# A gated attention and feed-forward kernel on one core: half sums, stores and loads become items of the hand-made lists, a left unit moves to another place, left rows of b share the home of left rows of x

## The chip, the cores and the metric

The kernel runs on one core of a Trainium2 chip. Its engines are TensorE (PE; its weight loads are shown apart as PEld), VectorE (DVE), ScalarE (ACT), GpSimd (POOL) and SyncE (SP), which here only issues DMAs. Each engine runs its own instructions in order, and semaphores join them. The metric is device time of one execution in microseconds (us), less is better; the median of three runs of the kernel before is 1715.51 us (1715.17 to 1721.14).

## What is computed

A sequence of 2048 rows of 640 numbers goes through two branches, and a gate for each row mixes them. Branch A is attention in 64 segments of 32 rows, each with 8 memory rows in front; the memory of a segment is what the segment before put out at its first 8 positions. So the segments form a chain. Branch B is a feed-forward block with a gated GELU.

```python
S, Dm, H, Dh, M, seg = 2048, 640, 32, 192, 8, 32
mem = mem0
for s in range(64):
    h = concatenate([mem, x[32*s:32*s+32]])          # 40 rows
    q, k, v = h @ Wq, h @ Wk, h @ Wv                 # 32 heads of 192
    p = softmax(mask(q @ k.T * scale))
    o = (p @ v) @ Wo                                 # 40 x 640
    mem, outs[s] = o[:8], o[8:]
a = concatenate(outs)
b = (gelu(x @ w_gate) * (x @ w_up)) @ w_down
g = sigmoid((x * gate_w).sum(-1))
result = g * a + (1 - g) * b
```

## The kernel before

**Feed-forward first.** Four blocks of 512 rows are computed before the attention. For each block `ffn_gu` runs 12 pairs of matmul groups, ACT does a GELU on each and DVE a product; `gate_block` computes the gate; `ffn_down` runs four row groups of 128. After each row group ACT and DVE move the result from PSUM to one of four buffers `brow`, and ACT issues one DMA that stores 128 rows of b in a scratch tensor in HBM (line 881). In this phase stores, and loads of the first x, are issued by ACT.

**Segments.** A segment has 24 new rows that nothing waits for ("first rows" of x), 8 memory rows from the segment before, and 8 last rows. The last 8 rows of four segments, a group, do not take part in the recurrence as queries of the next segment's memory, so they are the "left" rows: their q and k are computed for four segments at once ("left units", items `lf` and their copying out, `le`), stored in an HBM scratch (`lst store`, line 950, or in halves, line 955) and loaded again for each segment (`stg`, line 1000). Their attention outputs are kept in `uTl` and multiplied with Wo once for each group (`Wol`, at place 3). The four segments of a group are its places 0 to 3, and each place has its own list in `PROGS`.

**Lists.** A list names the order in which work is given to the engines. Heads are taken in four octets, in rising order at even and falling order at odd segments. `g` projects q, k or v of an octet, one of five 128-row pieces of the contraction at a time (each piece and matrix is four matmuls in four column tiles of PE); `tq`, `tk` transpose the rows of q and k on DVE after ACT took them out of PSUM; `sc` computes scores and gives DVE the maximum and the subtraction; `ex` is exp on ACT and sum, reciprocal and product on DVE; `pt` transposes the probabilities on PE; `pv` multiplies with v, and ACT (line 1265), for the last octet also DVE (line 1270), moves the result to `uT`; `wo` multiplies half an octet with Wo; `vb` projects v of the next group's left rows. All engines get their instructions in the order of the list, so an item's place decides what stands in front of what on each engine.

**The end of a segment.** The Wo products of octets 0 to 2 lie in a PSUM bank as two halves on different partitions. `half_sums` moves one half to SBUF on ACT (line 1289) and adds on DVE (two instructions, line 1292); it stands right behind the last of these products. When the last octet's products are done, DVE adds both parts (line 1468) and transposes the memory rows into the next segment's input (line 1472), and the first projection of the next segment waits for that.

**Left rows of u.** POOL copies the 8 left columns of each octet from `uT` to `uTl` (line 1273). So `uT` has 40 columns for each slot, and ACT takes 480 numbers (320 in the last octet) for each partition out of PSUM.

**Weights.** All weights of the attention do not fit in SBUF. Sixteen pairs of pieces share a home; each segment loads the partner of a piece after its use ("swap", line 645), thirteen pieces of 384 KB of Wq, Wk and Wv, one of them only in a part of `HX` bytes for each partition (line 642), and three of 480 KB of Wo. A load is used later in the same segment. All these, and the small loads and stores of a segment, go through SP in the order in which they were given: `out_store` (line 1021) and `x_load` (line 751) behind the last piece of k of octet 1, `bz_load` (line 1012) behind the last projection, four `bzl load` (line 1017), `outl` (line 1026) and so on.

**Names.** `bz` holds b, then the result, of a segment; `bzl` the same of a group's left rows; `XL` the left rows of x; `zpart` and `zsum` are the half sums.

A dependence is found by regions. For PSUM a reader also waits for readers of the same bank on other engines that were given before it.

Of the kernel before, what the change touches and what calls it, by code (L numbers as in the profile page):

```python
# [231 lines left out]
def _build(nc, A_x, A_mem0, A_Wq, A_Wk, A_Wv, A_Wo, seg_len, w_gate, w_up, w_down,  # L232
# [40 lines left out]
    b_scr = nc.dram_tensor("ffn_b_scratch", (S, Dm), BF, kind="Internal").ap()  # L273
    x_scr = nc.dram_tensor("x_scratch", (NSEG, 128, KT * XA), BF, kind="Internal").ap()
# [20 lines left out]
    wsB["bzl"] = al(DJ * 2)  # L295
# [5 lines left out]
    wsB["uT"] = al(NUB * 12 * R * 2)  # L301
# [101 lines left out]
    UB = 12 * R * 2  # L403
    uT = [bview(wsB_off["uT"] + b * UB, UB).rearrange("p (t c r) -> p t c r", c=3, r=R) for b in range(NUB)]
# [7 lines left out]
    bz, bzl = [bview(wsB_off[nm], DJ * 2) for nm in ("bz", "bzl")]  # L412
    Zt = PT[:, 0:DJ]
    r_bzlj = [sreg(wsB_off["bzl"], DJ * 2, 32 * j, 32 * j + 32) for j in range(4)]
# [4 lines left out]
    r_bz, r_bzl = [sreg(wsB_off[nm], DJ * 2) for nm in ("bz", "bzl")]  # L419
# [3 lines left out]
    fp_sz = {"xst": 16 * KT * XA * 2, "xls": 4 * KT * 64, "gr": 512, "gwT": 64}  # L423
# [7 lines left out]
    o_gr = fp_off["gr"]  # L431
# [36 lines left out]
    xls = bview(fp_off["xls"], fp_sz["xls"]).rearrange("p (g c) -> p g c", c=KT * 32)  # L468
    r_xls = sreg(fp_off["xls"], fp_sz["xls"])
    LSB = 4 * 2 * LW * 2  # L470
    lst_off = [fp_off["xst"] + i * LSB for i in range(3)] + [o_ul + 2 * UTQ]
    assert 3 * LSB <= fp_off["gr"] - fp_base
# [36 lines left out]
    def piece_view(key, o):  # L509
        if key[0] == 3:  # L510
# [872 lines left out]
    def segment(s):  # L1383
# [4 lines left out]
        for n, item in enumerate(PROGS[q]):  # L1388
# [57 lines left out]
            if item == gate_at[q]:  # L1446
                gate_now(s)
# [126 lines left out]
```

## Time and profile before

| | us |
|---|---|
| median of three runs | 1715.51 |
| profiled execution, device time | 1721.14 |
| its span, first to last instruction | 1719.3 |
| feed-forward phase and first left units | to about 180 |
| 64 segments | about 180 to 1715 |

The granted clock of TensorE was 0.996 of full speed over the span. The profile's page gives the busy time of each engine, the share of the DMA engines, the chain of waits, and groups of instructions with their mean duration and the idle time in front of them. A view of waits gives who waited for whom in total; a timeline gives instructions in order of time, equal neighbours merged; a view of windows gives busy time in stretches of the span. "ACTq" and "SPq" are the sequencers that issue DMAs. An engine's busy time in PE is modelled: matmuls are pipelined, and a matmul's shown duration is longer than the time after which the next one starts.

### The profile page before, as it was taken

To read this page: it belongs to the slowest core of one execution; us is meant where nothing else is said; L and a number is where in the kernel's file an instruction comes from. 1 tells how busy PE (TensorE), PEld (TensorE's weight loads), DVE (VectorE), ACT (ScalarE), POOL (GpSimd) and SP (SyncE) were. 2 spreads that over 40 slices of the span, in tenths; PEclk is the share of its full clock that TensorE was granted. 3 is DMA by queue.
4 is the path that set the end of the run, shared out by engine and by line. 5 is a ranking of instruction groups with operands and counts; after the bars stand their busy time and mean duration, and the time that the engine had idled before them with its cause. 6 is when DMAs were issued, how large, how long until landed. Compare 5 with 4: busy or idle time off the path is not lost. (4 is left out here: it accounts for less than half of the span.)

```text
span 1719.3 us, 80494 instructions
## 1 busy us (share of the span) xinstructions
PE 1592.6 (93%) x39181; PEld 825.5 (48%) x31501; DVE 956.2 (56%) x2930; ACT 801.1 (47%) x1899; POOL 415.7 (24%) x1101
## 2 busy tenths in 40 slices
PE   9999999999899989899999999899898999899987
PEld 4554445444544445454545445454445445454444
DVE  2222656656565655556565666556565656556554
ACT  3222454545454554545454544445454545445444
POOL 1100222222222222222222222222222222222222
PEclk9999999999999999999999999999999999999999
DMA  9914988978888788888788887879787887879876
GB/s 323 319 53 137 322 299 291 320 278 285 276 303 318 278 293 282 298 304 298 280 280 290 311 299 272 290 280 320 255 288 279 314 312 269 291 265 322 274 275 240
DMA packets 273822, 484.99 MB, mean 282 GB/s; under 512 B 107686, under 2 KB 142782, under 8 KB 273470
## 3 DMA queue, kind: packets, MB, share of 16 engines
q1 hardware_dynamic: 270414, 476.78, 79.2%
q8 instruction: 276, 4.52, 1.0%
q10 hardware_dynamic: 3056, 3.07, 0.5%
q14 instruction: 76, 0.62, 0.1%
HBM read 458.64 MB, written 21.10 MB: 279 GB/s over the span
## 5 line engine op out<-in xcount | busy, mean ns | idle before, releaser
L1121 PE MATMUL ps<-arena 128*32 128x384 bf16 x9940 | 710.8, 329 | 20.6 <-DVE arena L1472 11.8
L226 PE MATMUL ps<-arena 128*32 128x384 bf16 x7680 | 595.3, 327 | 14.3 <-ACT arena L1039 4.4
L1121 PEld LDWEIGHTS ps<-arena 128*32 128x32 bf16 x9940 | 254.7, 96 | 392.7 <-issue 260.6
L1155 DVE STREAM_TRANSPOSE arena<-arena 128x384 bf16<-128x384 bf16 x512 | 275.3, 561 | 151.4 <-ACT arena L1141 149.8
L1141 ACT ACTIVATE arena<-ps 128x384 bf16<-128x384 f32 x512 | 237.1, 490 | 227.0 <-PE ps L1121 212.2
L1283 PE MATMUL ps<-arena 128*32 128x320 bf16 x6144 | 279.7, 301 | 15.5 <-issue 13.2
L1273 POOL COPY arena<-arena 128x96 bf16<-128x96 bf16 x256 | 163.8, 640 | 527.8 <-ACT arena L1265 480.9
L1265 ACT ACTIVATE arena<-ps 128x480 bf16<-128x480 f32 (+1 forms) x256 | 137.5, 537 | 172.3 <-PE ps L1256 160.5
L1283 PEld LDWEIGHTS ps<-arena 128*32 128x32 bf16 x6144 | 169.3, 107 | 72.9 <-issue 23.8
L1006 POOL COPY arena<-arena 128x96 bf16<-128x96 bf16 x256 | 68.9, 269 | 485.4 <-PE ps L1176 387.4
L1144 ACT ACTIVATE arena<-ps 128x384 bf16<-128x384 f32 x256 | 125.2, 489 | 104.9 <-PE ps L1121 101.6
L1189 DVE TENSOR_REDUCE arena<-ps 104x4 f32<-104x160 f32 x256 | 82.8, 323 | 141.9 <-PE ps L1176 125.1
L1203 DVE TENSOR_REDUCE arena<-ps 104x4 f32<-104x160 f32 x256 | 80.9, 316 | 103.8 <-ACT ps L1201 101.5
L1239 ACT ACTIVATE arena<-ps 128x448 bf16<-128x448 f32 x192 | 104.1, 542 | 65.9 <-PE ps L1226 64.9
L1254 PE MATMUL ps<-arena 128*64 128x160 bf16 x1536 | 118.8, 243 | 7.3 <-ACT arena L941 3.2
L1201 ACT ACTIVATE ps<-ps 104x160 f32<-104x160 f32 x256 | 74.8, 292 | 103.0 <-DVE ps L1191 103.0
L1254 PEld LDWEIGHTS ps<-arena 128*64 128x64 bf16 x1536 | 79.8, 109 | 86.4 <-issue 29.9
L936 PE MATMUL ps<-arena 128*32 128x384 bf16 x1280 | 109.4, 327 | 1.1 <-issue 1.1
L1256 PE MATMUL ps<-arena 128*64 128x64 bf16 x1536 | 102.3, 193 | 0.0
L943 DVE STREAM_TRANSPOSE arena<-arena 128x384 bf16<-128x384 bf16 x128 | 73.0, 571 | 44.2 <-ACT arena L941 43.9
L1171 PE MATMUL ps<-arena 128*40 128x40 bf16 x2048 | 68.9, 182 | 26.4 <-DVE arena L1155 24.5
L1306 PE MATMUL ps<-arena 128*32 128x160 bf16 x3072 | 71.7, 233 | 21.7 <-DVE arena L1270 16.4
(85 smaller groups left out, 1824.2 us busy)
## 6 DMA issues: line engine op xcount, KB each, us to landing
arena<-in_A_Wk_dram SPq DMA_DIRECT2D x335, 384.0 KB, 6.7
arena<-in_A_Wv_dram SPq DMA_DIRECT2D x335, 384.0 KB, 8.3
arena<-in_A_Wo_dram SPq DMA_DIRECT2D x205, 480.0 KB, 5.4
arena<-in_A_Wq_dram SPq DMA_DIRECT2D x146, 384.0 KB, 5.2
arena<-left_qk_scratch SPq DMA_DIRECT2D x126, 96.0 KB, 2.1
left_qk_scratch<-arena SPq DMA_DIRECT2D x49, 192.0 KB, 2.8
arena<-in_A_Wq_dram SPq DMA_DIRECT2D x63, 144.0 KB, 3.4
left_qk_scratch<-arena SPq DMA_DIRECT2D x30, 96.0 KB, 3.3
```

What stands on the lines that cost most here:

```text
L226: return e.add_instruction(mybir.InstMatmult(name=nm, start_tensor_calc=like["start"], stop_tensor_calc=stop, tile_size=(128, 32), tile_po ...
L936: fns.append(lambda e, outp=outp, rhs=rhs, j=j: e.matmul(outp, lhs, rhs, start=(k == 0), stop=(k == KT - 1), tile_position=(0, 32 * j)))
L1121: fns.append(lambda e, outp=outp, rhs=rhs, j=j: e.matmul(outp, lhs, rhs, start=(k == 0), stop=(k == KT - 1), tile_position=(0, 32 * j)))
L1141: S_.add("act", lambda e, m=m, bk=bk: e.activation(out=rows_sb[m], in_=ps[:, bk, 0:384], func=ACTF.Copy), reads=[r_ps[bk]], writes=[r_rows ...
L1144: S_.add("act", lambda e, i=i, bk=bk: e.activation(out=v_sb[i % NVB].rearrange("p (c n) -> p c n", c=3), in_=ps[:, bk, 0:384].rearrange("p ...
L1155: S_.add("dve", lambda e: e.transpose(out=dst[:, :, 0:L], in_=rows_sb[m].rearrange("p (c r) -> p c r", r=L)), reads=[r_rows[m]], writes=[r ...
L1239: S_.add("act", lambda e: e.activation(out=PT, in_=ps[:, bank, 0:PTW + 128], func=ACTF.Copy), reads=[r_ps[bank]], writes=[r_PT], name="pT ...
L1254: return [lambda e: e.matmul(full, v[:, e0:e0 + 64], PTm[:, i], start=True, stop=False, tile_position=(0, 64 * i), skip_group_check=True), ...
L1256: lambda e: e.matmul(part, vl[:, e0:e0 + 64], PTl[:, i], start=False, stop=True, tile_position=(0, 64 * i), skip_group_check=True)]
L1265: S_.add("act", lambda e: e.activation(out=apx(u[:, 0, 0, :], [[R, na], [3 * R, 4], [1, R]]), in_=ps[:, A, 0:na * W].rearrange("p (c t r) ...
L1273: S_.add("pool", lambda e: e.tensor_copy(out=uTl[:, q, :, 12 * oc:12 * oc + 12].rearrange("p i (t c) -> p t c i", c=3), in_=u[:, :, :, L:R ...
L1283: fns.append(lambda e, i=i, t=t, j=j, gv=gv: e.matmul(ps[32 * j:32 * j + 32, bank, 0:2 * DJ].rearrange("p (h n) -> p h n", h=2), lhs2[i], ...
```

## The change

1. **uT and uTl.** `uT` keeps 32 columns; ACT takes 384 numbers (256 in the last octet) from PSUM. POOL's copy is gone; DVE copies the left columns from PSUM to `uTl` (96 numbers; in the last octet 64 and 32 from two banks).
2. **bzl in the home of XL.** `bzl` has no home of its own. It is loaded at place 3 behind `("g", 1, 4)`, and the next group's `XL` is loaded at place 0 behind the last projection, once the stores of `bzl` have landed. The left unit of octet 3, which place 0 worked on, is worked on at place 2.
3. **A scratch for left rows of b.** In the feed-forward phase ACT issues four more stores of 8 rows for each row group of 128; `bzl` is then loaded by one DMA in place of four.
4. **The memory that this frees**, with `xls` and the gate's row moved into `brow`, goes to the piece that is loaded in part: `HX` is 384 in place of 1152 bytes for each partition.
5. **New items.** `zp` and `zs` are the two parts of the half sums, `ou` the store of the segment before, `xt` the load of x, `bz` the load of b. `outl` stands at `("sc", 2)` of place 0.
6. **All four lists are new**, with the same kinds of work.

```diff
-    wsB["uT"] = al(NUB * 12 * R * 2)
+    wsB["uT"] = NUB * 12 * L * 2
...
-    HX = 1152
+    HX = 384
...
+            for i in range(4):
+                S_.add(AUXQ, lambda e, bs=bs, row0=row0, i=i: e.dma_start(
+                    bl_scr[row0 // 128, :, M * i:M * i + M].rearrange("j r n -> r j n"),
+                    brow[bs][L * i + XA:L * i + L].rearrange("t (j n) -> t j n", j=4)),
+                    reads=[r_brow[bs]], ..., name="bl store %d" % row0)
...
-    LUNIT = ({1: 3}, {0: 1, 1: 0}, {1: 2}, {})
+    LUNIT = ({}, {0: 1, 1: 0}, {0: 2, 1: 3}, {})
...
     def bzl_load(g):
-        for j in range(4):
-            S_.add(AUXQ, lambda e, j=j: e.dma_start(bzl[32 * j:32 * j + 32], rows(b_scr, g)[1][:, :, DJ * j:DJ * (j + 1)]),
+        S_.add(AUXQ, lambda e: e.dma_start(bzl, bl_scr[g].rearrange("j r n -> (j r) n")),
...
+        S_.add("act", lambda e: e.activation(out=u.rearrange("p t c r -> p c t r")[:, 0:na], in_=pa[:, 0:na, :, 0:L], func=ACTF.Copy),
+               reads=[r_ps[A]], writes=[ru[0]] if na == 2 else ru, name="uT evac s%d o%d" % (s, o))
         if na == 2:
-            S_.add("dve", lambda e: e.tensor_copy(out=u[:, :, 2, :], in_=ps[:, B, 2 * W:3 * W].rearrange("p (t r) -> p t r", r=R)),
+            S_.add("dve", lambda e: e.tensor_copy(out=u[:, :, 2, :], in_=pb[:, 2, :, 0:L]),
                    reads=[r_ps[B]], writes=[ru[1]], name="uT mid s%d o%d" % (s, o))
-        S_.add("pool", lambda e: e.tensor_copy(
-            out=uTl[:, q, :, 12 * oc:12 * oc + 12].rearrange("p i (t c) -> p t c i", c=3), in_=u[:, :, :, L:R]),
-            reads=[r_uT[o % NUB]], writes=[r_uTl[q][oc]], name="uTl s%d o%d" % (s, o))
+            S_.add("dve", lambda e: e.tensor_copy(out=ul[:, 2], in_=pb[:, 2, :, L:R]),
+                   reads=[r_ps[B]], writes=[r_uTl[q][oc]], name="uTl mid s%d o%d" % (s, o))
+        S_.add("dve", lambda e: e.tensor_copy(out=ul[:, 0:na], in_=pa[:, 0:na, :, L:R]),
+               reads=[r_ps[A]], writes=[r_uTl[q][oc]], name="uTl s%d o%d" % (s, o))
...
-            if n == nqkv:
-                bz_load(s)
-                if q == 2:
-                    bzl_load(g)
-                if q == 3 and g + 2 < NG:
-                    xl_load(g + 2, XL, r_XL, "xl0")
+                if q == 0 and 0 < g and g + 1 < NG:
+                    xl_load(g + 1, XL, r_XL, "xl0")
```

The new lists end, from the last octet's scores on, like this (place 0, 1, 2, 3):

```python
[..., ("g", 6, 0), ("wo", 0, 1), ("sc", 3), ("pt", 2), ("g", 6, 1), ("g", 6, 2), ("g", 6, 3), ("ex", 3), ("pv", 2), ("wo", 1, 0),
 ("wo", 1, 1), ("pt", 3), ("g", 6, 4), ("wo", 2, 0), ("bz", 0), ("wo", 2, 1), ("zp", 0), ("pv", 3), ("zs", 0), ("wo", 3, 0), ("wo", 3, 1)]
[..., ("wo", 0, 0), ("ex", 2), ("sc", 3), ("pv", 1), ("g", 6, 1), ("pt", 2), ("lf", 1, 1, 1), ("ex", 3), ("lf", 1, 1, 2), ("g", 6, 2),
 ("wo", 0, 1), ("pv", 2), ("lf", 1, 1, 3), ("pt", 3), ("g", 6, 3), ("g", 6, 4), ("lf", 1, 1, 4), ("le", 1, 1, 0), ("wo", 1, 0), ("wo", 1, 1),
 ("pv", 3), ("bz", 0), ("wo", 2, 0), ("le", 1, 1, 1), ("wo", 2, 1), ("wo", 3, 0), ("zp", 0), ("zs", 0), ("wo", 3, 1)]
[..., ("wo", 0, 1), ("sc", 3), ("pv", 1), ("pt", 2), ("lf", 2, 1, 3), ("g", 6, 0), ("g", 6, 1), ("lf", 2, 1, 4), ("g", 6, 2), ("ex", 3),
 ("g", 6, 3), ("wo", 1, 0), ("le", 2, 1, 0), ("pv", 2), ("g", 6, 4), ("bz", 0), ("wo", 1, 1), ("pt", 3), ("wo", 2, 0), ("wo", 2, 1),
 ("zp", 0), ("pv", 3), ("wo", 3, 0), ("zs", 0), ("le", 2, 1, 1), ("wo", 3, 1)]
[..., ("sc", 3), ("wo", 1, 0), ("ex", 3), ("g", 6, 0), ("xt", 0), ("g", 6, 1), ("bz", 0), ("g", 6, 2), ("pv", 2), ("g", 6, 3), ("vb", 0),
 ("g", 6, 4), ("wo", 1, 1), ("pt", 3), ("wo", 2, 0), ("pv", 3), ("vb", 1), ("wo", 2, 1), ("zp", 0), ("wo", 3, 0), ("wo", 3, 1), ("vb", 2), ("vb", 3), ("zs", 0), ("vb", 4)]
```

At place 2 the new list begins with a left unit of octet 2, `("xt", 0), ("lf", 2, 0, 0), ("lf", 2, 0, 1), ("g", 0, 0), ...`; what it puts out is stored from the part of `uTl` that belongs to places 2 and 3 (`lst[3]`), in front of the first `pv`. The old list of place 2 ended `("wo", 2, 1), ("pv", 3), ("le", 2, 1, 1), ("wo", 3, 0), ("wo", 3, 1)`, that of place 0 `("pv", 3), ("wo", 2, 0), ("le", 0, 1, 1), ("wo", 2, 1), ("wo", 3, 0), ("wo", 3, 1)`, with the half sums right behind `("wo", 2, 1)` in each.

More of the change, by code (lines that the diff above doesn't have):

```diff
@@ L294, in _build @@
     NVB, NUB = 2, 2
-    wsB["bzl"] = al(DJ * 2)
     wsB["K"] = al(12 * R * 2)
@@ L402, in _build @@
     SC = 512 - 4 * R
-    UB = 12 * R * 2
-    uT = [bview(wsB_off["uT"] + b * UB, UB).rearrange("p (t c r) -> p t c r", c=3, r=R) for b in range(NUB)]
+    UB = 12 * L * 2
+    uT = [bview(wsB_off["uT"] + b * UB, UB).rearrange("p (t c r) -> p t c r", c=3, r=L) for b in range(NUB)]
     r_uT = [sreg(wsB_off["uT"] + b * UB, UB) for b in range(NUB)]
@@ L411, in _build @@
     r_uTl = [[sreg(o_ul + UTQ * q_ + 192 * o_, 192) for o_ in range(NOCT)] for q_ in range(4)]
-    bz, bzl = [bview(wsB_off[nm], DJ * 2) for nm in ("bz", "bzl")]
+    o_bzl = wsA_off["XL"]
+    bz, bzl = bview(wsB_off["bz"], DJ * 2), bview(o_bzl, DJ * 2)
     Zt = PT[:, 0:DJ]
-    r_bzlj = [sreg(wsB_off["bzl"], DJ * 2, 32 * j, 32 * j + 32) for j in range(4)]
+    r_bzlj = [sreg(o_bzl, DJ * 2, 32 * j, 32 * j + 32) for j in range(4)]
     assert 2 * DJ * 4 <= wsB["rows"]
@@ L418, in _build @@
     r_zp = sreg(wsB_off["rows"], 2 * DJ * 4)
-    r_bz, r_bzl = [sreg(wsB_off[nm], DJ * 2) for nm in ("bz", "bzl")]
+    r_bz, r_bzl = sreg(wsB_off["bz"], DJ * 2), sreg(o_bzl, DJ * 2)
     r_Z = [Rg("z", i, i + 1) for i in range(2)]
@@ L422, in _build @@
     r_mem0r = sreg(wsB_off["uTl"], Dm * 2)
-    fp_sz = {"xst": 16 * KT * XA * 2, "xls": 4 * KT * 64, "gr": 512, "gwT": 64}
+    fp_sz = {"xst": 16 * KT * XA * 2, "gwT": 64}
+    o_xls, o_gr = [ffn_off["brow"] + b * Dm * 2 for b in (3, 2)]
+    assert 4 * KT * 64 <= Dm * 2 and NBR == 4
     fp_off = {}
@@ L1015, in bzl_load @@
     def bzl_load(g):
-        for j in range(4):
-            S_.add(AUXQ, lambda e, j=j: e.dma_start(bzl[32 * j:32 * j + 32], rows(b_scr, g)[1][:, :, DJ * j:DJ * (j + 1)]),
-                   reads=[Rg("dr", 128 * g, 128 * g + 128)], writes=[r_bzlj[j]], dma_sem="bzl%d" % j, name="bzl load g%d" % g)
+        S_.add(AUXQ, lambda e: e.dma_start(bzl, bl_scr[g].rearrange("j r n -> (j r) n")),
+               reads=[Rg("dbl", g, g + 1)], writes=[r_bzl], dma_sem="bzl", name="bzl load g%d" % g)
     def out_store(s):
@@ L1367, in left_evac @@
     def left_evac(s, u, m, n):
-        half = s % 4 == 2
+        half = s % 4 == 2 and u == 1
         if half and m:
             assert n > PROGS[s % 4].index(("pv", NOCT - 1))
+        if s % 4 == 2 and u == 0:
+            assert n < PROGS[2].index(("pv", 0))
         dst, rd = (lh[m], r_lh[m]) if half else (lst[3][:, :, m], r_lst[3])
@@ L1379, in left_sums @@
     def left_sums(g):
+        half_part(LB, "left g%d" % g)
         half_sums(LB, "left g%d" % g)
@@ L1396, in segment @@
                 proj(s, item)
-                ki = [j for m, j in GROUPS[i] if m == 1 and item[2] == KT - 1]
-                kind, i = ("k", ki[0]) if ki else ("", 0)
-                if kind == "k" and i == 1:
-                    if s > 0:
-                        out_store(s - 1)
-                    if s + 1 < NSEG:
-                        x_load(s + 1)
+            elif kind == "zp":
+                half_part(OB, "s%d" % s)
+            elif kind == "zs":
+                half_sums(OB, "s%d" % s)
+            elif kind == "ou":
+                if s > 0:
+                    out_store(s - 1)
+            elif kind == "xt":
+                if s + 1 < NSEG:
+                    x_load(s + 1)
+            elif kind == "bz":
+                bz_load(s)
             elif kind == "tq":
@@ L1412, in segment @@
                     left_sums(g - 1)
+                if i == 2 and q == 0 and g > 0:
+                    assert n < nqkv
+                    outl_store(g - 1)
             elif kind == "ex":
@@ L1482, in segment @@
             if s + 1 == NSEG:
+                half_part(LB, "left g%d" % g)
                 half_sums(LB, "left g%d" % g)
```

33 lines of the change are left out of this document (16 added, 17 removed), and 80 rows, old and new, of the table PROGS.

## Prediction

> **What bounds the kernel now.** I read the page first, then the waits of PE, then the windows of one segment at place 1, and last its timeline.
>
> ```profile
> span 1719.3 us, 80494 instructions
> PE 1592.6 (93%) x39181; PEld 825.5 (48%) x31501; DVE 956.2 (56%) x2930; ACT 801.1 (47%) x1899; POOL 415.7 (24%) x1101
> ```
>
> PE is the engine to follow: 93% busy, in one stream. The same work stays on it, so a gain can come only from its idle time, some 7%, and from time in which it looks busy but stands (a modelled end hides that). Who it waits for (total us, times, longest us):
>
> ```profile
> PE ps L1171 <- DVE arena L1155: 24.5, 46, 0.7
> PE ps L1306 <- DVE arena L1270: 16.4, 16, 1.1
> PE ps L1121 <- DVE arena L1472: 11.8, 19, 0.8
> PE ps L1221 <- DVE arena L1208: 8.5, 17, 0.7
> ...
> PE ps L1306 <- DMA arena<-in_A_Wo_dram: 2.5, 5, 0.8
> ```
>
> So: scores wait for transposed rows, the last octet's Wo for `uT`, a segment's first projection for the memory rows, `pt` for the softmax; 16 or 17 times means once in a group of four segments. Weights hardly show, but the windows (us; PE, PEld, DVE, ACT, POOL busy; clock; DMA share; GB/s) show how near they are:
>
> ```profile
> 304.85:308.85 4.00, 4.00 (x114) 1.49 (x70) 2.68 (x9) 2.50 (x7) 0.30 (x2) 1.00 0.96 323
> 308.85:312.85 4.00, 4.00 (x112) 2.01 (x90) 2.53 (x9) 2.82 (x7) 1.18 (x3) 1.00 1.00 382
> 312.85:316.85 4.00, 3.29 (x94) 1.99 (x82) 3.04 (x10) 1.67 (x4) 1.17 (x3) 1.00 1.08 387
> 320.85:324.20 3.35, 2.93 (x92) 1.60 (x76) 2.49 (x9) 1.43 (x4) 1.33 (x3) 1.00 0.31 80
> ```
>
> The swaps fill the DMA engines through the middle and leave them near idle at the end: a second bound just under the first. PE's idle time lies in the last third.
>
> **The change part by part**, for one group of four; there are 16.
>
> *Scores of the last octet.*
>
> ```profile
> 314.21 0.35 PE L1121 MATMUL ps<-arena 128*32 128x384 bf16 x4
> ...
> 315.76 0.28 PE L1171 MATMUL ps<-arena 128*40 128x40 bf16 x8 [0.71 <-DVE arena L1155]
> ...
> 320.68 1.00 PE L1283 MATMUL ps<-arena 128*32 128x320 bf16 x24
> 320.85 0.44 ACT L1265 ACTIVATE arena<-ps 128x320 bf16<-128x320 f32 x1 [0.64 <-PE ps L1256]
> 320.86 0.33 DVE L1270 CAST arena<-ps 128x160 bf16<-128x160 f32 x1
> 321.51 1.18 PE L1306 MATMUL ps<-arena 128*32 128x160 bf16 x48
> 321.73 0.44 ACT L1289 ACTIVATE arena<-ps 64x320 f32<-64x320 f32 x1
> 322.39 0.67 DVE L1292 TENSOR_TENSOR arena<-ps,arena 64x160 f32<-64x160 f32 x2
> 322.51 0.34 PE L936 MATMUL ps<-arena 128*32 128x384 bf16 x4
> 323.16 0.25 DVE L1468 TENSOR_TENSOR arena<-ps,arena 128x64 bf16<-128x64 f32 x1
> 323.44 0.25 DVE L1472 STREAM_TRANSPOSE arena<-arena 128x64 bf16<-128x64 bf16 x1
> 323.75 0.35 PE L1121 MATMUL ps<-arena 128*32 128x384 bf16 x4
> 323.92 0.34 PE L226 MATMUL ps<-arena 128*32 128x384 bf16 x4
> ```
>
> A piece of four matmuls shows 0.35 us but the next starts 0.16 later (323.75, 323.92). So k's last piece ended issuing at 314.37, and its scores started at 315.76: 1.39 us over ACT and DVE. Against that stands the PE work between, counted in the lists with 0.16 for a piece, 0.41 for a `wo` half (24 matmuls in 320.68 to 321.51 are two), 0.42 for a `pv` and 0.17 for a `pt` (my estimates from the starts). Old: 1.46, 0.39, 0.49, 1.14 us at places 0 to 3; place 1 has only one `pv` between. Loss 1.00 + 0.90 + 0.25 = 2.1. (The row's 24.5 for 46 waits leaves out some 0.18 of each that the modelled ends hide: 33 us, 2.1 for each of 16 groups, agrees.) New: 1.12, 1.06, 1.62, 0.97, so 0.27 + 0.33 + 0 + 0.42 = 1.0. **−1.1**.
>
> *Softmax at place 3.* `pt` waits for L1208 17 times, 8.5 us, with the hidden 0.18 about 0.6 to 0.7 in a group. The old distance from scores to `pt` is 1.62 there, the new one 2.59; nowhere in the new lists is it under 2.2, the 1.62 + 0.6 that is needed. **−0.6**.
>
> *Segment starts.* Behind the last Wo, DVE now does half sums (0.67), L1468 (0.25), L1472 (0.25), and only then comes the first projection. At the end above, 322.51 to 323.75 holds two left pieces (0.32): 0.9 lost. From place 3 to 0, `vb` covers it. With `zp` and `zs` ahead of the last `wo`, the losses 0.67, 0.88 and 0.83 (timelines) at the starts of places 1, 2 and 3 become 0.15, 0.56 and 1.18. The last gets worse: at place 2 DVE has both `uTl` copies, the `uT` copy, half sums 0.67 and the left transpose 0.58 in front of L1468. **−0.5**.
>
> *`pv` 3 next to `wo` 3.* From the end of `pv` (320.68) to the end of ACT's L1265 (321.29) and a hop of 0.08 is 0.69 us, which `wo` 2 covers at place 1. At place 2 nothing lies between, now or then; the old loss there was 16.4/16 = 1.0, with the hidden part 1.1, because the half sums stood ahead of L1270 on DVE. They move behind: 0.69. At place 0 `wo` 2 0 and 2 1 move ahead of `pv`: 0 to 0.69. **+0.3**. ACT's shorter reads (256 for 320 numbers) may take 0.06 off; the `zp` of 0.44 now stands ahead of L1265, but runs under the 0.42 of `pv`.
>
> *Smaller waits* (k of octet 1 and octet 3 at place 2, the mask, `pv` behind a late v) vanish at some places and appear at others: 0, with ±0.6 as bounds.
>
> *POOL's copy and what replaces it.*
>
> ```profile
> L1273 POOL COPY arena<-arena 128x96 bf16<-128x96 bf16 x256 | 163.8, 640 | 527.8 <-ACT arena L1265 480.9
> L1265 ACT ACTIVATE arena<-ps 128x480 bf16<-128x480 f32 (+1 forms) x256 | 137.5, 537 | 172.3 <-PE ps L1256 160.5
> ```
>
> POOL's 0.64 had no one waiting but the left Wo much later, so its going is worth nothing. ACT saves some 0.08 an octet, hidden under PE except beside `wo` 3. DVE gains five copies a segment; L1468's 64 numbers took 0.25, L1270's 160 0.33, so 96 take about 0.28: 1.4 us in 24 for an engine 56% busy. It hides in DVE's idle time; where it doesn't is counted above. But DVE runs in order, and the first copy at place 2 has a new wait: `uTl` of places 2 and 3 is the store's source for the left unit that moved there (`lst[3]`), so the copy stands until that store has landed, and behind it stand all row transposes, maxima and softmax steps, on which PE waits.
>
> ```profile
> left_qk_scratch<-arena SPq DMA_DIRECT2D x49, 192.0 KB, 2.8
> arena<-in_A_Wk_dram SPq DMA_DIRECT2D x335, 384.0 KB, 6.7
> ...
> 308.70 0.74 SPq L950 DMA_DIRECT2D left_qk_scratch<-arena  x1
> DMA to landing us min/median/max: 8.4/8.4/8.4
> ```
>
> In the new list SP issues it about 5.5 us behind the first projection, `pv` 0 comes at about 11.4, and DVE has some 0.9 us in hand. Most old stores started at a segment's end, on idle queues: 2.8. The one in mid-segment took 8.4. At 5.5 us the queues hold mostly k weights: I take their 6.7, landing at 12.2, **+0.2**; bounds 2.8 (0) and 8.4 to 9 (about 2).
>
> *Swaps.* `HX` takes 768 x 128 bytes from each segment's loads: 98 KB at 382 GB/s, 0.26 us. The chain gains come to 1.1 + 0.6 + 0.5 − 0.3 = 1.9 a group, 0.48 a segment, and the last Wo piece landed just in time already (issue, what waited for it, landing):
>
> ```profile
> L645 SPq DMA_DIRECT2D arena<-in_A_Wo_dram x1: 328/328/328, 317.4 to 317.4; - x1
>   PEld ps L1306: 0.2, 1
> DMA to landing us min/median/max: 4.9/4.9/4.9
> ```
>
> So 0.22 a segment, 0.9 a group, is not covered. It binds where a piece landed with nothing in hand, and not where the queues ran dry; I take half: **+0.4**, bounds 0 and 1.9 (all gains eaten). `bzl` in one load saves three issues on SP, with nothing behind them on the path: 0. `XL` is now loaded about 17 us into place 0, behind the last swap; it lands in 4.9 or so, about 1 us before the left unit that opens place 1 needs it: 0, at a cost of the excess if that cover is gone.
>
> Sum −1.1 − 0.6 − 0.5 + 0.3 + 0.2 + 0.4 = −1.3; 16 x −1.3 = **−21 us**.
>
> *Feed-forward.* ACT issues 64 more stores, four behind each b store.
>
> ```profile
> L881 ACTq DMA_DIRECT2D ffn_b_scratch<-arena x16: 326/346/350, 40.6 to 171.4; - x16
> L1026 ACTq DMA_DIRECT2D out_dram<-arena x2: 756/766/777, 1715.6 to 1716.4; - x2
> 46.14 0.60 ACT L875 ACTIVATE arena<-ps 128x512 bf16<-128x512 f32 x1 [2.66 <-PE ps L870]
> 49.40 0.60 ACT L875 ACTIVATE arena<-ps 128x512 bf16<-128x512 f32 x1 [2.66 <-PE ps L870]
> 50.35 0.33 ACTq L881 DMA_DIRECT2D ffn_b_scratch<-arena  x1
> 51.69 0.60 ACT L855 ACTIVATE arena<-ps 128x512 bf16<-128x512 f32 x1 [1.69 <-PE ps L852]
> 53.52 1.24 PE L849 MATMUL ps<-arena 128*128 128x512 bf16 x5
> ```
>
> A row group comes every 3.26 us; ACT ends with it 1.3 us after L875 starts. Four issues cost 4 x 0.35 by L881, 4 x 0.77 by L1026, whose shape (one row strip in pieces) is nearer. I take 0.5: 2.0, a cycle of 3.3 that just holds. At a block's end the stores and two x loads put the GELU of 51.69 off by some 2 us; it has until 53.52 (PE's next use of the bank), less its 0.6. So PE loses 1 to 2 us at three borders and 1 at the transition: **+5**; bounds 1 (0.35) and 14 (0.77, with the cycle at 4.4).
>
> In sum −16 of the profiled 1721.1, its span of 1719.3 and 1.8 around it: 1705. That run lies 5.6 above the median of 1715.5, so I forecast **1699**.
>
> **The rivals.**
>
> *All chain gains hold.* If the DVE wait and the swap landings cost nothing, 16 x −1.9, or −31, and the feed-forward term at 3.5: 1688. For it: five weight waits in the whole trace. Against: the DMA share of 1.0 in mid-segment.
>
> *The swaps are the bound.* Loads then set the end of each segment and the gains turn into waits for weights; only the +5 stays: 1721. For it: windows at 1.0 and 1.08, and the 0.2 that L1306 waits. Against: 0.31 in the last window, and the 98 KB.
>
> *DVE stands at place 2 (the other side).* The store lands like that of 308.70: 5.5 + 8.8 = 14.3 against 12.3, 2.0 us in each group, +32 for the −24 that the other terms give, and +5: 1728. It decides from a landing later than 12.3 us behind the first projection. For it: the 1.00 around 308.7 and the 8.4 row. Against: 5.5 us in, the queue has had less time to fill (0.96 at 304.85 to 308.85).
>
> *Stores are cheap to issue.* The feed-forward term is 0, so 1694. For it: only that ACT is idle 2.66 us before each L875. Against: L881's own 0.346 us for one store, 64 times 22 us of ACT, and the 0.766. The Trainium skill, "DMA: Bandwidth & Descriptors", section "Issuing engines are not separate DMA queues", says that the time a sequencer takes to start a DMA is usually small relative to the DMA itself; the L1026 and L881 rows speak against leaning on it, since what counts here is the engine's queue behind the issue and not the transfer.
>
> **How the numbers follow.** Chances: forecast 0.38 (its own range 1684 to 1712), all gains 0.16, swaps 0.18, DVE stands 0.21, cheap stores 0.07. What can be told from no change is about 0.5%, 8.6 us. Faster: 0.33 of the forecast's, 0.16 and 0.07, in all 0.56; same: 0.05 of the forecast's and 0.11 of the swaps', 0.16; slower: 0.07 of the swaps' and 0.21, 0.28. The range goes from 1672 (all gains, with smaller waits at −0.6: 16 x −2.5, feed-forward at its lower bound, and ACT's 0.06 beside `wo` 3 at four places, 16 x 0.24) to 1740 (DVE stands, feed-forward nearer 14).
>
> **What would show it.** Right: L1171's wait for L1155 at about half of 24.5; L1221's for L1208 near nothing; L1306's for `uT` twice a group at 0.5 or so; L1121's for L1472 fewer, the longest at place 3's start. Wrong: DVE idle before a `uTl` copy, released by a DMA; PE waits for weights of far over 2.5 us; ACT's GELU at a block's end more than 3 us late; group time not near 95 us.

## The result and the profile after

The changed kernel takes 1806.4 us (median of four runs, 1794.81 to 1809.94) against 1716.14 us for the kernel before, a ratio of 1.0501 (95% interval 1.0468 to 1.0534): 5% slower. The forecast was 1699, its range ended at 1740. The page of the changed kernel (span, busy time, the chain that ended last by line) begins:

```profile
span 1802.3 us, 80466 instructions
PE 1603.6 (89%) x39162; PEld 828.9 (46%) x31501; DVE 1067.3 (59%) x3250; ACT 780.9 (43%) x1899; POOL 251.3 (14%) x845
PE ps L1128 19%; PE ps L226 13%; PE ps L1291 9%; DMA arena<-in_A_Wv_dram 7%; DMA ffn_bl_scratch<-arena 5%; DMA arena<-in_A_Wo_dram 4%; PE ps L1261 3%; PE ps L854 3%; PE ps L851 3%; PE ps L944 2%; PE ps L1183 2%; PE ps L1170 2%; DMA arena<-in_A_Wq_dram 2%; PE ps L1316 2%; DVE arena L1302 2%
```

The span is 83.0 us longer. One line of the chain belongs to an item of the change: the new stores of the feed-forward phase, 5% of the span. Where the loss begins and ends is told by the stores of b themselves (a view of one source line: duration in ns, first and last start in us):

```profile
L883 ACTq DMA_DIRECT2D ffn_b_scratch<-arena x16: 349/349/379, 40.6 to 250.2; - x16
```

Before, the same 16 stores ran from 40.6 to 171.4. So 78.8 of the 83.0 us are lost before the attention begins; at the end of the first segment, when the memory rows are first transposed, it is 83.1 (289.0 in place of 205.9 us). The timeline of ACT shows how (start, us, engine, line; in brackets the idle time and who ended it):

```profile
39.63 0.60 ACT L877 ACTIVATE arena<-ps 128x512 bf16<-128x512 f32 x1 [1.33 <-PE ps L872]
40.65 0.35 ACTq L883 DMA_DIRECT2D ffn_b_scratch<-arena  x1
41.03 14.78 ACTq L887 DMA_DIRECT2D ffn_bl_scratch<-arena  x4
55.86 0.60 ACT L877 ACTIVATE arena<-ps 128x512 bf16<-128x512 f32 x1 [15.63 <-DMA ffn_bl_scratch<-arena]
```

Four new stores stand on ACT's queue for 14.78 us, though a single one takes some 0.3 us to issue. The next row group's L877 comes 16.2 us after the last, and not 3.26. This is the worst case: the first two row groups stand for 14.8 and 14.6 us, while the DMA engines were nearly full (shares of 1.04 and 0.94), and most of the later ones for some 4.5. The reason is in the code of the change. All four stores of a row group name the same region of the new scratch:

```python
reads=[r_brow[bs]], writes=[Rg("dbl", row0 // 128, row0 // 128 + 1)], dma_sem="bl%d%d" % (bs, i), ...
```

A write behind a write to one region is a dependence, so stores 2 to 4 each wait on ACT until the store ahead has landed, and everything behind them on ACT waits too. PE follows within two row groups, when both pairs of PSUM banks are full (waits of PE, total us, times, longest):

```profile
PE ps L869 <- DVE arena L880: 21.4, 4, 10.9
PE ps L851 <- ACT arena L877: 19.8, 5, 9.7
...
PE ps L226 <- DVE arena L880: 8.2, 1, 8.2
PE ps L851 <- ACT arena L857: 6.6, 3, 3.2
```

That is 56 of the 78.8 us. Nearly all of the rest is PE itself, which was busy 22 us longer at a lower clock; the last section shows this.

For the segments, the waits of PE answer to those shown of before (lines have moved by 7 to 16; L1183 is the part of the scores over 64 rows, which goes first where a `pv` stands right behind `sc`; before it was L1171, the part over 128, that waited):

```profile
PE ps L1128 <- DVE arena L1488: 24.1, 37, 1.3
PE ps L1316 <- ACT arena L1046: 16.4, 32, 0.5
PE ps L1228 <- DVE arena L1215: 13.1, 28, 0.7
PE ps L1183 <- DVE arena L1162: 7.7, 8, 2.1
PE ps L1316 <- DMA arena<-in_A_Wo_dram: 6.7, 15, 0.7
PE ps L1233 <- DMA arena<-in_A_Wv_dram: 4.0, 11, 0.9
PE ps L1128 <- DMA arena<-in_A_Wk_dram: 3.7, 7, 1.0
PE ps L1128 <- DMA arena<-in_A_Wv_dram: 3.5, 8, 0.6
PE ps L226 <- DMA arena<-in_A_Wq_dram: 2.9, 5, 0.9
```

The second row is the last octet's Wo, which waits for `uT` (L1275). The view names L1046, a copy of the gate that ACT does right behind L1275, but the code has no such wait, and in the timeline L1275 ends at 286.23, L1316 starts at 286.29 and L1046 ends at 286.30.

The scores' wait fell from 24.5 to 7.7 us; those for memory rows (11.8 before) and for the softmax (8.5 before) grew, and weights, which showed little before, now cost PE about 21 us. Behind the last store of b the kernel takes 1802.3 − 250.2 = 1552.1 us, before 1719.3 − 171.4 = 1547.9: the segments gained nothing in these two profiles. The result therefore has two questions: whether the chained stores are the whole loss, and where the 21 us went that were forecast for the segments.

### The profile page after: what moved, and what is told of

Same layout as the page of the kernel before. It is cut to its first block, busy times and chain, and to the rows that moved or that the text cites. A ratio compares the mean times of both kernels' runs of the same rounds, so it can differ in the third digit from the quotient of the medians.

```text
span 1802.3 us, 80466 instructions
## 1 busy us (share of the span) xinstructions
PE 1603.6 (89%) x39162; PEld 828.9 (46%) x31501; DVE 1067.3 (59%) x3250; ACT 780.9 (43%) x1899; POOL 251.3 (14%) x845
## 4 chain that ended last, share of the span: by engine, by line
PE 62%; DMA 19%; DVE 10%; issue 5%; ACT 3%; ACTq 1%; POOL 0%; DVEq 0%; POOLq 0%
PE ps L1128 19%; PE ps L226 13%; PE ps L1291 9%; DMA arena<-in_A_Wv_dram 7%; DMA ffn_bl_scratch<-arena 5%; DMA arena<-in_A_Wo_dram 4%; PE ps L1261 3%; PE ps L854 3%; PE ps L851 3%; PE ps L944 2%; PE ps L1183 2%; PE ps L1170 2%; DMA arena<-in_A_Wq_dram 2%; PE ps L1316 2%; DVE arena L1302 2%
## 5 line engine op out<-in xcount | busy, mean ns | idle before, releaser
L1128 PE MATMUL ps<-arena 128*32 128x384 bf16 x9940 | 715.5, 331 | 40.5 <-DVE arena L1488 24.1
L1128 PEld LDWEIGHTS ps<-arena 128*32 128x32 bf16 x9940 | 258.9, 97 | 420.3 <-issue 262.6
L1148 ACT ACTIVATE arena<-ps 128x384 bf16<-128x384 f32 x512 | 237.2, 490 | 223.0 <-PE ps L1128 205.8
L1291 PE MATMUL ps<-arena 128*32 128x320 bf16 x6144 | 272.2, 300 | 9.3 <-issue 9.0
L1291 PEld LDWEIGHTS ps<-arena 128*32 128x32 bf16 x6144 | 174.8, 107 | 57.6 <-issue 18.6
L1282 DVE CAST arena<-ps 128x96 bf16<-128x96 f32 (+1 forms) x256 | 146.2, 571 | 86.7 <-PE ps L1291 23.8
L1275 ACT ACTIVATE arena<-ps 128x384 bf16<-128x384 f32 (+1 forms) x256 | 118.6, 463 | 173.1 <-PE ps L1263 157.6
L1014 POOL COPY arena<-arena 128x96 bf16<-128x96 bf16 x256 | 69.4, 271 | 661.7 <-PE ps L1183 456.7
L1151 ACT ACTIVATE arena<-ps 128x384 bf16<-128x384 f32 x256 | 125.0, 488 | 79.0 <-PE ps L1128 74.7
L949 ACT ACTIVATE arena<-ps 128x384 bf16<-128x384 f32 x128 | 62.9, 492 | 77.1 <-PE ps L944 51.2
L1316 PE MATMUL ps<-arena 128*32 128x160 bf16 x3072 | 73.6, 233 | 25.5 <-ACT arena L1046 16.4
```

What stands on the lines that cost most here:

```text
L1128: fns.append(lambda e, outp=outp, rhs=rhs, j=j: e.matmul(outp, lhs, rhs, start=(k == 0), stop=(k == KT - 1), tile_position=(0, 32 * j)))
L1148: S_.add("act", lambda e, m=m, bk=bk: e.activation(out=rows_sb[m], in_=ps[:, bk, 0:384], func=ACTF.Copy), reads=[r_ps[bk]], writes=[r_rows ...
L1151: S_.add("act", lambda e, i=i, bk=bk: e.activation(out=v_sb[i % NVB].rearrange("p (c n) -> p c n", c=3), in_=ps[:, bk, 0:384].rearrange("p ...
L1275: S_.add("act", lambda e: e.activation(out=u.rearrange("p t c r -> p c t r")[:, 0:na], in_=pa[:, 0:na, :, 0:L], func=ACTF.Copy), reads=[r_ ...
L1282: S_.add("dve", lambda e: e.tensor_copy(out=ul[:, 0:na], in_=pa[:, 0:na, :, L:R]), reads=[r_ps[A]], writes=[r_uTl[q][oc]], name="uTl s%d o ...
L1291: fns.append(lambda e, i=i, t=t, j=j, gv=gv: e.matmul(ps[32 * j:32 * j + 32, bank, 0:2 * DJ].rearrange("p (h n) -> p h n", h=2), lhs2[i], ...
```

## The experiments

### The stores

**Own regions.** Only the regions change, not the stores:

```diff
-                    ... writes=[Rg("dbl", row0 // 128, row0 // 128 + 1)], ...
+                    ... writes=[Rg("dbl", row0 // 32 + i, row0 // 32 + i + 1)], ...
-               reads=[Rg("dbl", g, g + 1)], ...
+               reads=[Rg("dbl", 4 * g, 4 * g + 4)], ...
```

> The changed kernel, but the four stores of 8 rows declare four different parts of the scratch, so none waits for the one before. Theory (each store stands on ACT until the one before has landed, 4 to 5 us each, 81 us in all before segment 0): the first segment starts near 180 instead of 258 us and the time falls to 1724 to 1732. Rival (such small stores are slow in themselves, 10 KB in rows of 320 bytes): ACT or the DMA queue stays behind, the time stays over 1770.

Measured: 1715.43 us, ratio to before 0.9986 (0.9958 to 1.0014). Timeline of ACT, and the stores of b, in this kernel:

```profile
39.68 0.60 ACT L877 ACTIVATE arena<-ps 128x512 bf16<-128x512 f32 x1 [1.35 <-PE ps L872]
40.70 0.35 ACTq L883 DMA_DIRECT2D ffn_b_scratch<-arena  x1
41.09 1.41 ACTq L887 DMA_DIRECT2D ffn_bl_scratch<-arena  x4
42.94 0.60 ACT L877 ACTIVATE arena<-ps 128x512 bf16<-128x512 f32 x1 [2.66 <-PE ps L872]
...
L883 ACTq DMA_DIRECT2D ffn_b_scratch<-arena x16: 349/349/363, 40.7 to 172.6; - x16
```

The same four stores now take 1.41 us of ACT, 0.35 each, and a row group again 3.26 us. What cost the time was not the issue but the landing, for which each store held ACT up (14.78 us for four stores against 1.41). The time lies under what was expected, by about 9 us, since the feed-forward phase loses 1.2 us and not 5 and the segments are a little faster than in the profile of the changed kernel.

**The kernel before, with the stores.** The 64 stores of the change are added to it, and nothing else.

```diff
+            for i in range(4):
+                S_.add(AUXQ, lambda e, bs=bs, row0=row0, i=i: e.dma_start(bl_scr[...], brow[bs][...]),
+                    reads=[r_brow[bs]], writes=[Rg("dbl", row0 // 128, row0 // 128 + 1)], dma_sem="bl%d%d" % (bs, i), ...)
```

> The kernel before with nothing but the 64 stores added, as the change has them (nobody reads what they store). Theory (the chained stores are the loss): 1716 + 75 to 85, so 1790 to 1801. Rival (the loss is that of the new lists or of the lower clock they bring): at most 1725.

Measured: 1798.42 us, ratio 1.0458 (1.0429 to 1.0487).

```profile
L882 ACTq DMA_DIRECT2D ffn_b_scratch<-arena x16: 349/349/350, 41.2 to 252.5; - x16
```

By the medians the old lists with the chained stores lose 80 us, the changed kernel 90, with intervals that meet; with own regions 91 of these are gone. The first question is answered from both sides.

**The old load.** The changed kernel without the stores; `bzl` comes in four DMAs from the scratch of b, as before.

```diff
-        S_.add(AUXQ, lambda e: e.dma_start(bzl, bl_scr[g].rearrange("j r n -> (j r) n")), ...
+        for j in range(4):
+            S_.add(AUXQ, lambda e, j=j: e.dma_start(bzl[32 * j:32 * j + 32], rows(b_scr, g)[1][:, :, DJ * j:DJ * (j + 1)]), ...
```

> The changed kernel without the 64 stores; bzl is loaded by four DMAs from the scratch of b, as before. What is left is the segments' part of the change. By the two profiles a group of four takes 96.0 us in both kernels: 1714 to 1724. By the sum of the prediction (-1.3 a group, nothing in the feed-forward phase): 1695. If the stores were not the loss: over 1780.

Measured: 1715.24 us, ratio 0.998 (0.9959 to 1.0002). So the one load in place of four is worth nothing that can be measured, as the prediction had it, and the segments' part of the change is about −3 us (−7 to 0 by the interval), not −21.

### The segments

**The lists alone.** As the run before this, with POOL's copies, `uT` of 40 columns, a home for `bzl`, and `HX` 1152.

```diff
-    wsB["uT"] = NUB * 12 * L * 2
+    wsB["uT"] = al(NUB * 12 * R * 2)
+    wsB["bzl"] = al(DJ * 2)
-    HX = 384
+    HX = 1152
-        S_.add("dve", lambda e: e.tensor_copy(out=ul[:, 0:na], in_=pa[:, 0:na, :, L:R]), ...
+        S_.add("pool", lambda e: e.tensor_copy(out=uTl[...], in_=u[:, :, :, L:R]), ...
```

> As the run with the old load, and also with POOL's copies of the left columns (uT 40 wide), bzl in a home of its own, HX 1152: the new lists and items alone. If DVE's copies of 0.6 us, twice what the prediction gave them, ate the gain of the lists: 10 to 20 us under the run with the old load, near 1700. If the swap loads ate it: the 98 KB that each segment loads again cost up to 16 us, 1725 to 1736. Both at once: near the run with the old load.

Measured: 1734.75 us, ratio 1.0094 (1.0069 to 1.0118), 19 us over the run with the old load, as the theory of the swap loads had it. But its trace names something else:

```profile
PE ps L1285 <- POOL arena L1275: 20.5, 13, 2.3
...
279.38 0.64 POOL L1275 COPY arena<-arena 128x96 bf16<-128x96 bf16 x1 [0.16 <-POOL arena L1058]
280.08 0.64 PE L1285 MATMUL ps<-arena 128*32 128x320 bf16 x12 [1.46 <-POOL arena L1275]
```

The left Wo of place 3 waits for POOL's last copy, 20.5 us in all. The copy takes 0.64 us, but that is not all: its input was there at 277.59, and it stood behind POOL's scaling of `bzl` (L1058), as it did in all 13 cases, beginning 0.6 to 2.6 us after its input. So in the new lists `wo_left` comes too soon for a copy that stands in POOL's order. PE's waits for weights are about the same as in the run with the old load (23.9 against 25.3 us). The number matched a theory that the profile does not bear out; the run says nothing on the loads' bytes.

**The kernel before with 98 KB less.** That was tried by itself: the piece that is loaded in part brings 384 bytes for each partition, and the rest of it keeps what was there, so some products use other weights.

```diff
-            S_.add("sp", lambda e: e.dma_start(bview(o, HX), piece_src(key)[:, c0:c0 + HX // 2]), ...
+            S_.add("sp", lambda e: e.dma_start(bview(o, 384), piece_src(key)[:, c0:c0 + 192]), ...
```

> The kernel before, but the piece that is loaded in part brings 384 in place of 1152 bytes for each partition; the rest of it keeps what was there, so some of the products use other weights. It prices the memory that the change frees, on the old lists: if the swap loads bound the old kernel, 0.26 us x 63 = 16 us less, 1701; if its own chain does, 1714 to 1718. The run without Wo's loads took 15 us off with fifteen times the bytes, so 1 to 5 us less is what I expect.

Measured: 1724.07 us, ratio 1.0035 (1.0011 to 1.0059): no gain, if anything a loss of some 5 us, which stays unexplained. The DMA part of the page:

```profile
arena<-in_A_Wq_dram SPq DMA_DIRECT2D x63, 48.0 KB, 3.1
```

With 144 KB the same load landed in 3.4 us. A third of the bytes is hardly sooner, and on the old lists the 0.26 us a segment that the prediction worked out from 98 KB at 382 GB/s did not come. The old lists wait little for weights; on the new ones `HX` was not tried by itself.

**The copies on DVE.** The kernel with own regions, with another order of the loops.

```diff
-        ul = uTl[:, q, :, 12 * oc:12 * oc + 12].rearrange("p i (t c) -> p c t i", c=3)
+        ul = uTl[:, q, :, 12 * oc:12 * oc + 12].rearrange("p i (t c) -> p i t c", c=3)
-        ... out=ul[:, 0:na], in_=pa[:, 0:na, :, L:R]
+        ... out=ul[:, :, :, 0:na], in_=pa[:, 0:na, :, L:R].rearrange("p c t r -> p r t c")
```

> The kernel with own regions (1715 us), with another order of the loops in DVE's copies of the left columns: 24 neighbouring bytes are written one after the other, where the change writes single numbers 96 bytes apart. Theory (the copies cost 0.61 us for 96 numbers because of how they write, and stand before what PE waits for): their mean falls to 0.3, and the time by 5 to 20 us, to 1695 to 1710. Rival (the copies hide in DVE's idle time): their mean falls, the time stays within 1710 to 1720. If the order makes no difference to a copy: 0.6 and 1715.

Measured: 1712.21 us, ratio to before 0.9953 (0.9925 to 0.9982). The groups of DVE by shape (count, then busy us, mean ns, idle time ahead), first with own regions alone:

```profile
L1282 DVE CAST arena<-ps 128x96 bf16<-128x96 f32 x192 | 116.7, 608 | 71.2 <-PE ps L1291 19.0 <-PE ps L1128 15.9 <-PE ps L1233 7.5
```

and with the other order, with the wait for the memory rows (24.0, 36 times, with own regions alone):

```profile
L1282 DVE CAST arena<-ps 128x96 bf16<-128x96 f32 x192 | 48.5, 253 | 82.2 <-PE ps L1128 22.5 <-PE ps L1291 18.4 <-PE ps L944 13.7
...
PE ps L1128 <- DVE arena L1488: 16.1, 26, 0.9
```

The copy falls from 608 to 253 ns, near the 0.28 us of the prediction, and 8 us of waits for the memory rows go. The time falls by 3 us, a difference that the two intervals leave open: most of the copies did hide.

**The softmax of place 3.** First octet 2's was moved, on the kernel with own regions:

```diff
- ("sc", 2), ("tq", 3), ("g", 5, 3), ("pv", 1), ("wo", 0, 0), ("ex", 2), ("g", 5, 4),
+ ("sc", 2), ("tq", 3), ("ex", 2), ("g", 5, 3), ("pv", 1), ("wo", 0, 0), ("g", 5, 4),
```

> The kernel with own regions, with one item of place 3 moved: the softmax of octet 2 behind the q rows of octet 3 and ahead of pv 1, where the change has it behind pv 1 and a wo half. Theory (the transposes of the probabilities wait 0.7 to 0.8 a group because exp stands on ACT behind the uT of pv 1, not because the list has too little between sc and pt): that wait goes to nearly 0, and the time falls by 8 to 12 us, to 1703 to 1707. Rival (the chain from scores to probabilities itself is 3.4 us long now): the wait stays at 0.7, 1715.

Measured: 1714.83 us, ratio 0.9972 (0.9949 to 0.9996); L1228's wait for L1215 is 12.9 us (27 times), 12.3 with own regions alone. A miss: the large wait belonged to octet 1. That octet's softmax was moved next:

```diff
- ("sc", 1), ("pv", 0), ("ou", 0), ("g", 3, 3), ..., ("g", 4, 3), ("ex", 1), ("g", 4, 4),
+ ("sc", 1), ("ex", 1), ("pv", 0), ("ou", 0), ("g", 3, 3), ..., ("g", 4, 3), ("g", 4, 4),
```

> The kernel with own regions, with the softmax of octet 1 at place 3 moved to right behind its scores, where the change has it eleven items later, behind the rows of octet 2. The run before this moved octet 2's and took away that octet's wait of 0.24 us; the large wait (0.7 to 0.8 us a group) belongs to octet 1. Theory (the wait comes from where exp stands in the list, not from a longer chain): L1228's wait for L1215 falls from 12.3 us to 3 or less, the group's place 3 loses 0.5 to 0.7 us. If this reaches the end: 1704 to 1707; if the swap loads take it back: 1710 to 1715.

Measured: 1710.84 us, ratio 0.9943 (0.9912 to 0.9974). The wait that it was to remove:

```profile
PE ps L1228 <- DVE arena L1215: 3.3, 11, 0.5
```

From 12.3 to 3.3 us: the wait came from where `ex` stands in the list. Of the 9 us some 5 reach the median, a difference that the two intervals leave open.

**Without Wo's swap loads.** A fifth of a segment's bytes is left out, in both kernels; half of Wo's products then use other weights.

```diff
         loaded[slot_id[key]] = key
+        if key[0] == 3 and name != "res":
+            return
```

> The kernel with own regions, without the swap loads of Wo: three loads of 480 KB in each segment are left out, a fifth of its bytes, so half of Wo's products use other weights. Theory (weights that land late eat the gain of the new lists): PE's waits for DMAs (some 26 us) go, and the time falls by 20 to 30 us, to 1685 to 1695. Rival (weights cost little): over 1707.

> The kernel before, without the swap loads of Wo (left out as in the run beside it). Theory (the old lists hardly waited for weights, 4 us in the trace): at most 8 us faster, 1708 to 1716, so that the new lists, with the weights out of the way, lead by 15 us or more. Rival (the weights held up both lists alike): it falls by as much as the run beside it, and the two stay within 6 us.

Measured: 1688.06 us on the new lists (ratio 0.9824, 0.9785 to 0.9864) and 1703.25 on the old (0.9914, 0.9885 to 0.9944). Both expectations were half right. The new lists fall by 27 us, as was expected, but PE's waits for DMAs did not go: they are 14.4 us, 24.4 with own regions alone. The old lists fall by 15 us and not by 8 at most, far more than their waits for Wo in the trace (2.5 us) would give. With these loads out of the way the new lists lead by 15.2 us, with them by about 3 (1715.43 against 1718.44). So by the medians, of 15 us that the change saves in the segments, some 12 are taken back once all weights are loaded; the intervals of the four ratios leave some 10 us either way on this 12. Which step takes them back is not shown: of the 27 us, the 10 that left PE's waits for DMAs are all that can be read as such.

**The left transpose of place 2.** With own regions, it was put behind the memory rows.

```diff
- ("wo", 3, 0), ("zs", 0), ("le", 2, 1, 1), ("wo", 3, 1)]
+ ("wo", 3, 0), ("zs", 0), ("wo", 3, 1), ("le", 2, 1, 1)]
```

> The kernel with own regions, with the last left transpose of place 2 behind the memory rows, where the change has it ahead. Theory (DVE's work ahead of the memory rows sets the start of place 3): L1128's wait for L1488 falls from 24.0 to about 15 us, and the time by 0.5 us x 15 = 8, to 1707, or less by what the swap loads take back. Rival (the last Wo products or ACT are what comes last): 24 and 1715.

Measured: 1738.71 us, ratio 1.012 (1.0071 to 1.0169), which neither theory had. Waits of PE and of SP's queue:

```profile
PE ps L1128 <- DMA arena<-in_A_Wk_dram: 30.0, 46, 2.2
PE ps L1128 <- DVE arena L1488: 20.3, 40, 1.0
...
SPq L963 <- DVE arena L951: 106.7, 30, 6.6
```

and of SP's queue with own regions alone:

```profile
SPq L963 <- DVE arena L951: 43.8, 16, 3.4
SPq L963 <- DVE arena L1484: 34.9, 14, 2.7
```

The wait for the memory rows did fall, from 24.0 to 20.3 us. But the stores of these left rows (L963) stand on SP until the late transpose is done, 106.7 us in 30 waits where it was 78.7 in 30, and twice as long at worst. Behind them stand the first k loads of place 3, which PE then waits for: 30.0 us in place of 4.7.

**The moves together.** First the other loop order, both softmax items and the late transpose at once, on own regions.

> Own regions, the other order in DVE's copies, both softmax items of place 3 earlier and the left transpose late, all at once. If the gains reach the end: 1715 - 3 - 10 - 8, near 1695. If the swap loads are the bound by now, as the two runs without Wo's loads suggest: 1702 to 1710, with PE's waits for DMAs over 30 us.

Measured: 1727.17 us, ratio 1.0045 (1.0021 to 1.0069): the late transpose spoils it. Then without it:

> Own regions, the other order in DVE's copies, and both softmax items of place 3 earlier; the left transpose stays where the change has it. If the small gains of the single runs (3 for the copies, 4 to 5 for the softmax) add up: 1702 to 1708. If the swap loads take them back: 1708 to 1714, with PE's waits for DMAs grown past those of the run with own regions.

Measured: 1706.94 us (12 runs), ratio 0.9936 (0.9912 to 0.9959), with these waits left:

```profile
PE ps L1128 <- DVE arena L1488: 17.6, 28, 0.9
PE ps L1128 <- DMA arena<-in_A_Wk_dram: 7.1, 13, 1.3
PE ps L1316 <- DMA arena<-in_A_Wo_dram: 6.7, 14, 0.8
PE ps L226 <- DMA arena<-in_A_Wq_dram: 5.8, 12, 1.2
```

The gains add up in the main, and this version is ahead of both kernels, of the one before by 0.6% (0.4 to 0.9) and of the changed one by 5.5%. PE's waits for weights are a little longer than with own regions alone (Wk 4.7, Wq 2.8 there; 26.9 against 24.0 us in all).

## Why the prediction was wrong

**The failed step: the feed-forward phase.** The prediction took the 64 stores as so many issues, "four issues cost 4 x 0.35 by L881, 4 x 0.77 by L1026", chose 0.5 us each, and came to +5 with bounds of 1 and 14. Each bound was a price for issuing, and none for waiting. The step that was left out is the dependence that the change writes down: four stores into one region wait for one another. The issue itself costs 0.35 us, L881's own price; without the waits the phase loses 1.2 us, and with them 78.8. The two lines were in the new function, the rule that a dependence is found by regions was known, and the same question was asked of another new DMA (the store that `uTl` at place 2 waits for). It was not asked of these. The rival in which the stores are cheap to issue was right about issuing and beside the point.

**Scores of the last octet (−1.1 a group): right.** 24.5 us of waits in 46 became 7.7 in 8, less than the half that was foreseen, and these eight have another cause, told below at place 2. (By the prediction's own prices the new list of place 0 holds 0.99 us of PE work and not 1.12, so the term should have read −1.0.)

**Softmax of place 3 (−0.6): wrong.** The prediction counted PE work from the scores to `pt`, 2.59 us, and held 2.2 for enough. But exp and the sums are given to ACT and DVE where `ex` stands in the list, and the new list puts it behind the rows of the next octet. The wait grew from 8.5 to 13.1 us; with `ex` behind its scores it is 3.3.

**Segment starts (−0.5): wrong.** The wait for the memory rows grew from 11.8 to 24.1 us. That the start of place 3 gets worse was foreseen (10.1 became 15.7 us, in 16 waits each); those of places 1 and 2 were to get better, and went from 1.7 to 8.4. The copies that stand ahead were priced at 0.28 us for 96 numbers; these took 0.61, and the last octet's two 0.46 and 0.30. With the faster copies of the other loop order (0.25 for 96) the wait is 16.1, still not a gain.

**`pv` 3 next to `wo` 3 (+0.3): right.** 16 waits of up to 1.1 us became 32 of up to 0.5, twice a group at 0.5, as foreseen (the 0.69 of the prediction less the 0.18 that a wait hides).

**The DVE wait at place 2 (+0.2): the wait was there, its price mis-sized.** The view of DVE's waits in the changed kernel puts only two down to the store, 4.1 us in all:

```profile
DVE arena L1282 <- DMA left_qk_scratch<-arena: 4.1, 2, 2.9
...
left_qk_scratch<-arena SPq DMA_DIRECT2D x49, 192.0 KB, 7.7
```

The timeline says otherwise. One store of place 2, its time to landing, the first copy behind it on DVE, and the scores of the last octet:

```profile
411.64 0.43 SPq L958 DMA_DIRECT2D left_qk_scratch<-arena  x1
DMA to landing us min/median/max: 8.4/8.4/8.4
...
420.19 0.61 DVE L1282 CAST arena<-ps 128x96 bf16<-128x96 f32 x1 [3.12 <-PE ps L1291]
422.19 0.27 PE L1183 MATMUL ps<-arena 64*40 64x40 bf16 x8 [1.61 <-DVE arena L1162]
```

The store lands at 420.04 and the copy starts at 420.19, though its `pv` had ended at 416.62; the view names a PE instruction that ended meanwhile. In all 15 groups that have this store the copy starts within 0.15 us of the landing, 1.6 to 4.1 us behind its `pv`, with DVE idle just before it for 34 us in all. The stores land after 6.5 to 8.9 us (median 8.1), later than the 6.7 that were assumed and near the 8.4 of the rival in which DVE stands. So DVE did stand there, as that rival has it; but PE waits for it in eight groups only, out of nine in which the copy comes 2.3 us or more behind its `pv`, and these are the eight waits of L1183, 7.7 us in all. That is 0.5 a group and not the rival's 2.0: DVE has some 2 us in hand, not 0.9. The same copies stand on the same landing with own regions and in the last version, where PE waits 2.5 and 1.7 us for it.

**Swaps (+0.4 a group, 6 us): right in kind, too small.** By the two runs without Wo's loads they took back some 12 of 15 us. The prediction's upper bound, all gains eaten, was nearly the case, and the 98 KB that were to soften it brought nothing on the old lists. Its rival "the swaps are the bound" comes nearest to the segments: without the chain of stores 1715 was measured, closer to its 1721 than to 1699. But the softmax and the segment starts lost time too, which that rival does not have.

**POOL's copy (0): right for the old lists only.** With the new ones, putting it back costs PE 20.5 us of waits, since it stands behind another step of POOL.

So the mechanism of the segments was half right, their sum (−21) should have been about −3, and the loss came from a place that the prediction had valued at +5.

## What to carry to other kernels

When a change adds DMAs, read which regions they declare before pricing their issue: a chain of waits on the queue of an engine that also computes costs the landing of each, many times its issue. Count the distance of a softmax or a transpose from where its list gives it to the engine, not from where its input is ready. Where transfers run just under the compute, price a gain by running both versions with some transfers left out, and look on each in-order queue for what stands behind a step that is moved later. And when a wait has several causes, compare the landing of each DMA with the start of the instruction: the view of waits names one cause only.

## What the runs showed of the hardware

After a long stall TensorE did not come back at full speed here. Windows of the changed kernel, over the rest of the feed-forward phase and around its first stall (us; PE, PEld, DVE, ACT, POOL busy; clock; DMA share; GB/s), two matmuls of one shape from its timeline, and last the feed-forward phase of the kernel before:

```profile
40.00:250.00 210.00, 152.76 (x886) 71.30 (x860) 31.18 (x56) 33.22 (x57) 10.30 (x22) 0.85 0.37 126
...
46.00:57.00 11.00, 0.12 (x3) 0.04 (x2) 0.29 (x1) 0.60 (x1) 0.00 (x0) 0.63 1.03 414
57.00:62.50 5.50, 5.50 (x21) 2.64 (x22) 0.00 (x0) 0.00 (x0) 0.00 (x0) 0.51 1.03 411
62.50:63.10 0.60, 0.57 (x4) 0.15 (x2) 0.00 (x0) 0.00 (x0) 0.00 (x0) 1.00 1.02 410
...
57.48 0.63 PE L869 MATMUL ps<-arena 128*128 128x512 bf16 x1
62.63 0.38 PE L869 MATMUL ps<-arena 128*128 128x512 bf16 x1
...
40.00:171.40 131.40, 131.00 (x846) 65.74 (x832) 31.59 (x56) 33.56 (x57) 10.34 (x22) 1.00 0.52 176
```

For 5.5 us behind an 11 us stall the granted clock was 0.51, and the matmul took 0.63 in place of 0.38 us. Over the whole phase the clock was 0.85 and PE was busy 152.76 us, where the kernel before took 131.00 at a clock of 1.00 for nearly the same matmuls: this is how 56 us of waits become a loss of 79. A short wait leaves no such mark: the prediction's window around the 0.71 us wait for the scores has a clock of 1.00. How long a stall it takes was not worked out.

The DVE copy of 96 numbers took 608 ns when it wrote single 2-byte numbers 96 bytes apart and 253 ns when it wrote 24 neighbouring bytes at a time; the reads differ between the two as well, so how much belongs to the writes was not settled. And a swap load of 48 KB landed in 3.1 to 3.3 us where one of 144 KB took 3.4.
